# Zero fills by DMA, a wider yield rule for GpSimd, weights in small pieces, and other seeds in a planned attention kernel

## The chip, the cores and the metric

The kernel runs on one core of a Trainium2 chip. A core has five engines that run their own instruction streams and meet only at semaphores: TensorE (PE, matrix products), VectorE (DVE), ScalarE (ACT), GpSimd (POOL) and SyncE (SP, which here only issues DMAs). TensorE writes its results to PSUM, which has eight banks of 128 partitions by 512 floats. The metric is the device time of one launch in microseconds, taken as the median of several runs. A shorter time is better.

## The reference, cut to what matters

One sequence of S = 2048 rows of width D = 512 is normalised, goes through an attention with 32 query heads of width 16 over one shared key and value head, and through a two-layer network with F = 1792; the two results are multiplied and added to the input:

```python
xn = _layernorm(x)                                   # x = A_x, 2048 x 512
q, k, v = xn @ wq, xn @ wk, xn @ wv                  # 32 heads of 16; one k and one v head
p = softmax(einsum("bhqd,bkd->bhqk", q, k) * 16 ** -0.5)
s = einsum("bhqk,bkd->bhqd", p, v) @ wo
g = silu(silu(xn @ w1) @ w2)
out = x + s * g
```

The scores are 32 x 2048 x 2048 numbers. Each needs an exponential, and neither scores nor probabilities ever leave the chip's local memories.

## The kernel before, in words

**Units of work.** Queries are cut into four chunks of 512 columns, and keys into 32 blocks of 64. A *unit* is the score tile of one key block against one chunk of queries for four heads, 128 partitions by 512 columns, in one PSUM bank. There are 32 groups of 64 units, 2048 units in all. The matrix products run on quarters of the array: four matmuls of 64 x 32 weights run side by side and fill half of the array, so the planner speaks of two *lanes*. One such foursome is called a *half* here. Scores (L966, and L960 where the loaded weights are used again) go to lane 1. The products of probabilities with values (L1302), called PV here, take lane 0. Those of the network, of the queries and of the output (L704) use halves of both lanes.

**Two ways to take an exponential.** A unit goes one of two ways. In the *A way*, ScalarE computes exp straight out of PSUM, one unit or two neighbouring banks at a time (L1666), and the unit needs one PV entry. In the *D way*, VectorE turns the score into the bits of an approximate exponential in bf16 with one multiply and add (L1041), eight units make a batch, and three shifted copies of the batch are made with an integer addition on GpSimd (L1224) or, where allowed, on VectorE (L1220). The four versions are averaged by the weights in the values, so such a unit needs four PV entries. Two entries of the two column halves share one half-slot of lane 0.

**Prologue.** x arrives in four parts of four row tiles. VectorE computes the statistics (L538, L542), an inverse square root by a few small operations (L555 to L564) and the normalised tile xn (L567). TensorE transposes it (L606), ScalarE or VectorE copies it out (L616, L617), and keys (L632, evacuated at L650) and values (L669, evacuated at L678) follow for each part. Scores can only use keys that have been evacuated, and D units start only when all keys are there. The keys exist a second time, shifted by 16 rows (`kt_sb[:, 1]`), for the odd groups, and the queries a second time, shifted by 32 rows (`qt_sb[:, r, 1]`). The shifts are DMAs within local memory (L1348 on GpSimd's queue, L714 on SP's), and what they leave uncovered must be zero. The zeros come from GpSimd: four memsets of 128 x 512 (L500) and one of 16 x 2048 (L496). GpSimd also writes the constant columns of the values (L494). A tile of zeros for warming up TensorE is made by VectorE (L477) in the fourth output buffer.

**The order of the work** comes from a planner that runs when the kernel is built. Every operation is a task with an engine, an assumed duration, keys that it reads and writes, a priority and sometimes a gate. The planner keeps a clock for each engine, always advances the engine that is furthest behind, and lets it take the best task that is ready. What it places is fixed in that order in the engine's instruction stream, and waits are added for each dependency. TensorE has its own rule (`pe_step`), which weighs the backlog of ScalarE against that of VectorE to decide whether the next unit goes the A way or the D way. Its parameters are drawn anew for every 6 us of planned time from a list of seeds (`SEEDS`, `Mix.draw`); seed 0 means no deviation. A different list gives a different order everywhere.

**The shared port.** VectorE and GpSimd operations that are marked `ports=2` are never planned at the same time: the planner makes each wait for the last one of the other engine (`last2`, `locked`). In `avail`, GpSimd's two-port tasks also step back when a two-port VectorE task is about to be ready, but only if that task has no gate (`d.gate is None`):

```python
                if d.ports == 2 and d.gate is None and all(p.op is not None for p in d.preds) and (
                        self.ready(DV, d.reads, d.writes) <= self.clk[PO] + HOLD_PO):
                    return None
```

The xn operations (L567) have a gate: a tile may be overwritten only when the tile four before it has been transposed. The shifted copies on VectorE (L1220) have one too.

**Weights.** `w1` comes in one DMA after the sixth xn tile, `w2` in four DMAs and `wo` in one, each after a certain product of the network has been planned (`later`, `hidden`). All go through SP's queue.

Of the kernel before, what the change touches and what calls it, by code (L numbers as in the profile page):

```python
# [15 lines left out]
P = 128  # L16
# [3 lines left out]
W1_AT, SKIP = 5, 1877.999  # L20
T_ISSUE, T_SWDGE = 450.0, 1000.0
J_BASE, J_END, MIXJ = 0.114, 1.312, 2
SEEDS, STRETCH = [0, 0, 882634, 0, 348373, 328499, 78780, 554384, 89101, 903077, 320169, 0, 878569, 280070, 102111, 381856, 427096, 265022, 0, 740569, 0, 0, 0, 191854, 393933, 374197, 266972, 0, 665170, 0, 882882, 218695, 9227, 955074, 159633, 731624, 518155, 138034, 620799, 357599, 376984, 365473, 457970, 796664, 668429, 641664, 991272, 0, 0, 23990, 593814, 88565, 504692, 394759, 276845, 267858, 882770, 104810, 721623, 135503, 603776, 0, 337714, 100793, 638616, 0, 419715, 752789, 751312, 664693, 308960, 0, 762547, 276261, 218757, 897693, 0, 624478, 290921, 0, 713781, 335568, 417921, 100939, 814701, 0, 180062, 99721, 614963, 258262, 411291, 131548, 802432, 314922, 883804, 569039, 54637, 401726, 110613, 0, 983842, 914345, 0, 0, 0, 0, 0, 0, 0, 0], 6000.0
# [5 lines left out]
HOLD_PO = 394.351  # L29
# [3 lines left out]
Q_URG = 0.404  # L33
J_SLIP = 1.014
NEXT_OB, OB_SLACK = 8, 67.243
# [22 lines left out]
WIDE, PAIR_WAIT, GRP_WAIT = 2, 17.474, 124.091  # L58
Q_LEAD = 3.566
A_HIGH, D_HIGH, SLACK = 1856.266, 2005.987, 50.146  # L60
LEAD, CROWD, FRAG, DB_LOW = 296.727, 0.54, 0.993, 1
RUN, HOLD, PRESS = 6, 411.985, 18
ROOM = 1
START_Z, START_H, AHEAD, NEAR = 10, 14, 0.206, 11
CLOSING, URGENT, END_DV = 0, 4.336, 58
STARVED = 543.663
JLATE, JEVAC = 1.132, 1
MATE = 176.663
# [7 lines left out]
class Task:  # L76
    __slots__ = ("eng", "dur", "emit", "reads", "writes", "prio", "preds", "op", "on_place", "dma", "gate", "ports", "after", "ring", "first")

    def __init__(self, eng, dur, emit, reads=(), writes=(), prio=5, preds=(), on_place=None, dma=0, gate=None, ports=1):
        self.ports, self.after, self.ring = ports, None, None  # L80
        self.eng, self.dur, self.emit = eng, dur, emit
        self.reads, self.writes, self.prio = tuple(reads), tuple(writes), prio
        self.preds, self.on_place, self.dma, self.gate = [p for p in preds if p is not None], on_place, dma, gate
        self.op = None
# [11 lines left out]
class Planner:  # L96
# [122 lines left out]
    def avail(self, task):  # L219
# [5 lines left out]
        if task.eng == PO and task.ports == 2:  # L225
            for d in self.tasks[DV]:
                if d.ports == 2 and d.gate is None and all(p.op is not None for p in d.preds) and (
# [124 lines left out]
def bass_recurrent_scan__grouped_kv_mqa__dense_activation_silu__prompt_kernel(  # L352
# [29 lines left out]
    with ExitStack() as es:  # L382
# [75 lines left out]
        dma(SP, "wq", wq_sb[:], A_wq.rearrange("(dc p) n -> p dc n", p=P), 512, ["wq"], prio=0)  # L458
        for j in range(1, 4):
            dma(SP, "x", ds_sb[:, XB + 4 * j // BS, 4 * j % BS * NQ:(4 * j % BS + 4) * NQ].bitcast(BF16).rearrange("p (t d) -> p t d", d=D),  # L460
                xv[:, 4 * j:4 * j + 4, :], 512, [xkey(4 * j + h) for h in range(4)], prio=1)
        def later(task, which):
# [8 lines left out]
        for k, (f0, f1) in enumerate(((0, 4), (4, 8), (8, 11), (11, 14))):  # L471
            later(dma(SP, "w2", w2_sb[:, f0:f1, :], w2v[:, f0:f1, :], 128 * (f1 - f0), [("w2", k)], prio=3), hidden(0, k))
        wov = A_wo.rearrange("(o p) n -> p o n", p=P)
        later(dma(SP, "wo", wo_sb[:], wov, 512, ["wo"], prio=4), hidden(0, 4))

        pl.add(Task(DV, 60.0, lambda v: v.memset(scr_sb[:], 0.0), (), ["scr"], -1))
        pl.add(Task(DV, 550.0, lambda v: v.memset(zer_sb, 0.0), (), [("ob", 3)], 0))  # L477
# [15 lines left out]
        for j in range(K + 1):  # L493
            pl.add(Task(PO, T_MS, lambda g, j=j: g.memset(v_sb[:, j, :, DH:], 1.0 if j == 0 else SHIFT_W[j - 1]),  # L494
                        (), [("Vw", j)], 2, ports=2, gate=lambda: ("st", 0) in pl.lastw and ("st", 3) not in pl.lastw or xn_task[3].op is not None))
        pl.add(Task(PO, 1800.0, lambda g: g.memset(kt_sb[0:DH, 1, :], 0.0), [("xn", 3)], [("kt1", c) for c in range(NC)], 3,  # L496
                    gate=lambda: all(xn_task[t].op is not None for t in range(4)), ports=2))
        q1_fill = {}
        for r in range(NQR):
# [1275 lines left out]
```

## Time and profile before

| what | us |
|---|---|
| median of three runs (659.71 to 660.05) | 659.73 |
| the profiled execution | 660.8 |
| its span, first to last instruction | 658.8 |
| busy: TensorE, ScalarE, VectorE, GpSimd | 649.1, 641.5, 640.4, 571.2 |
| first exponential of the A way starts | 11.48 |
| first D evacuation on VectorE starts | 39.12 |
| last exponential ends | 649.1 |
| last output DMA is issued | 655.2 |

Three engines are busy for 97% of the span or more, so a share of busy time tells little. What counts is in which stretch each of them sits idle, and who it waits for then. The profile's matmul ends are modelled, so TensorE's busy time includes time in which only one of its lanes works. In the listings, the number in square brackets is the idle time of the engine ahead of the row, with what ended it. TensorE's clock was granted in full throughout.

### The profile page before, as it was taken

Reading aid. Unit: us, or ns where it says so; the run is one execution under the profiler, and the core shown is the slowest. Engines: PE = TensorE matmul, PEld = TensorE weight load, DVE = VectorE, ACT = ScalarE, POOL = GpSimd, SP = SyncE. Lnnn points to the kernel's source line nnn. Section 1 sums busy time; section 2 is a strip of 40 time slices with the busy share of each in tenths; the row PEclk is TensorE's granted clock in tenths of the full one; section 3 lists DMA queues with packets and bytes.
Section 4 is the critical chain, followed back from the end, with each engine's and each line's share of the span. In section 5 each row is a group of like instructions: output and inputs, shape, how many; then the busy total and the mean of one; then the engine's idle time right before and its main releaser. Section 6 shows DMA issues by size and latency. Waiting matters only on the chain.

```text
span 658.8 us, 44466 instructions
## 1 busy us (share of the span) xinstructions
PE 649.1 (99%) x22182; PEld 332.3 (50%) x19438; DVE 640.4 (97%) x1169; ACT 641.5 (97%) x1128; POOL 571.2 (87%) x320
## 2 busy tenths in 40 slices
PE   8999999999999999999999999999999999999997
PEld 3445555544555554544555554454445555554543
DVE  8999999999999999999999999999999999999976
ACT  6989999999999999999999999999999999999995
POOL 4038799999998978999999878999999998889891
PEclk9999999999999999999999999999999999999999
DMA  5314100000000010000000010000000000100001
GB/s 177 129 48 121 42 4 4 10 5 10 5 10 20 28 34 5 10 4 5 10 4 11 21 36 26 4 5 10 4 10 4 10 21 20 34 13 5 4 4 34
DMA packets 13432, 15.91 MB, mean 24 GB/s; under 512 B 2112, under 2 KB 12608, under 8 KB 13248
## 3 DMA queue, kind: packets, MB, share of 16 engines
q1 hardware_dynamic: 12768, 12.36, 6.2%
q8 instruction: 162, 2.65, 1.7%
q0 software_dynamic: 192, 0.46, 0.2%
q10 hardware_dynamic: 288, 0.26, 0.1%
q14 instruction: 22, 0.18, 0.1%
HBM read 8.95 MB, written 2.10 MB: 17 GB/s over the span
## 4 chain that ended last, share of the span: by engine, by line
PE 89%; ACT 5%; DVE 3%; POOL 1%; DMA 0%; issue 0%
PE ps L966 29%; PE ps L1302 24%; PE ps L704 21%; PE ps L960 14%; ACT pa_sb L1666 4%; DVE stats_sb L538 1%; DVE xn_sb L567 1%; PE ps L1510 0%; ACT t_sb L760 0%; DVE xnT_sb L617 0%; DMA kt_sb<-kt_sb 0%; POOL qt_sb L500 0%; POOL kt_sb L496 0%; DVE v_sb L678 0%; DVE kt_sb L650 0%
## 5 line engine op out<-in xcount | busy, mean ns | idle before, releaser
L1666 ACT ACTIVATE pa_sb<-ps 128x512 bf16<-128x512 f32 (+1 forms) x1038 | 610.6, 762 | 5.4 <-PE ps L966 4.4
L1224 POOL INT64_ADD ds_sb<-db_sb x300 | 562.2, 1897 | 43.7 <-DVE db_sb L1041 33.7
L1041 DVE TENSOR_SCALAR db_sb<-ps 128x512 uint16<-128x512 f32 x808 | 500.6, 679 | 5.5 <-PE ps L960 2.0
L966 PE MATMUL ps<-qt_sb,kt_sb 64*32 64x512 bf16 x5448 | 473.7, 378 | 1.9 <-DVE v_sb L678 0.8
L1302 PE MATMUL ps<-ds_sb,v_sb 64*32 64x512 bf16 x4848 | 352.1, 377 | 0.1
L1302 PE MATMUL ps<-pa_sb,v_sb 64*32 64x512 bf16 x2480 | 271.3, 377 | 0.7 <-DVE v_sb L678 0.5
L960 PE MATMUL ps<-qt_sb,kt_sb 64*32 64x512 bf16 x2744 | 265.7, 375 | 0.0
L966 PEld LDWEIGHTS ps<-qt_sb,kt_sb 64*32 64x32 bf16 x5448 | 132.3, 89 | 161.4 <-ACT pa_sb L1666 68.8
L1302 PE MATMUL ps<-db_sb,v_sb 64*32 64x512 bf16 x1616 | 211.8, 377 | 0.0
L1302 PEld LDWEIGHTS ps<-ds_sb,v_sb 64*32 64x32 bf16 x4848 | 134.1, 91 | 44.4 <-issue 15.8
L704 PE MATMUL ps<-xnT_sb,w_sb 64*32 64x512 bf16 x1792 | 135.4, 377 | 0.0
L704 PE MATMUL ps<-w_sb,u_sb 64*32 64x512 bf16 x1792 | 133.7, 376 | 0.0
L1302 PEld LDWEIGHTS ps<-pa_sb,v_sb 64*32 64x32 bf16 x2480 | 92.0, 91 | 28.2 <-issue 8.4
L1302 PEld LDWEIGHTS ps<-db_sb,v_sb 64*32 64x32 bf16 x1616 | 66.8, 91 | 16.5 <-issue 5.9
L704 PEld LDWEIGHTS ps<-xnT_sb,w_sb 64*32 64x32 bf16 x1792 | 43.8, 91 | 24.0 <-issue 6.5
L704 PEld LDWEIGHTS ps<-w_sb,u_sb 64*32 64x32 bf16 x1792 | 44.8, 91 | 20.3 <-issue 6.1
L760 ACT ACTIVATE t_sb<-ps 128x512 bf16<-128x512 f32 x72 | 47.8, 664 | 0.0
L761 DVE SCALAR_TENSOR_TENSOR u_sb<-t_sb,ps 128x512 bf16<-128x512 bf16 x56 | 37.9, 677 | 1.0 <-ACT t_sb L760 1.0
L704 PE MATMUL ps<-xnT_sb,wq_sb 64*32 64x512 bf16 x480 | 37.6, 378 | 0.0
L704 PE MATMUL ps<-wo_sb,on_sb 64*32 64x512 bf16 x384 | 30.8, 377 | 0.0
L1319 DVE STREAM_TRANSPOSE ps<-ps 128x512 f32<-128x512 f32 (+1 forms) x33 | 23.2, 705 | 3.3 <-PE ps L1302 3.3
L1348 POOL DMA_DIRECT2D kt_sb<-kt_sb x4 | 2.3, 566 | 21.2 <-DVE rstd_sb L558 7.8
(75 smaller groups left out, 193.4 us busy)
## 6 DMA issues: line engine op xcount, KB each, us to landing
xr_sb<-in_A_x_dram SPq DMA_DIRECT2D x16, 128.0 KB, 2.3
out_dram<-ob_sb SPq DMA_DIRECT2D x16, 128.0 KB, 1.7
w_sb<-in_B_w_dram SPq DMA_DIRECT2D x1, 1792.0 KB, 7.2
ds_sb<-in_A_x_dram SPq DMA_DIRECT2D x3, 512.0 KB, 6.6
qt_sb<-qt_sb SPq DMA_DIRECT2D x16, 96.0 KB, 2.5
w_sb<-in_B_w_dram SPq DMA_DIRECT2D x2, 512.0 KB, 4.7
w_sb<-in_B_w_dram SPq DMA_DIRECT2D x2, 384.0 KB, 3.3
wq_sb<-in_A_wq_dram SPq DMA_DIRECT2D x1, 512.0 KB, 4.8
```

What stands on the lines that cost most here:

```text
L538: ts_ = pl.add(Task(DV, 593.0, lambda v, t=t: v.bn_stats(stats_sb[:, t, :], x_tile(t)), [xkey(t)], [("st", t)], 1 + j, gate=(lambda j=j: S ...
L567: xn_task[i] = pl.add(Task(DV, 323.0, lambda v, i=i: v.tensor_scalar(xn_sb[:, i % 4, :], x_tile(i), mv_sb[:, i, 0:1], rstd_sb[:, i:i + 1], ...
L704: h = pe.matmul(bank(b)[32 * j:32 * (j + 1), :], lhsT=lhs(k, rows, 32 * j, 32), rhs=rhs(k, rows), start=first, stop=last, tile_position=(r ...
L760: t1 = Task(AC, T_AF + 0.8333 * NQ, lambda a: a.activation(t_sb[:, k, :], bank(b), ACT.Tanh, scale=scale), [("ps", b)], [("t", k)], 0)
L761: t2 = Task(DV, T_P, lambda v: v.scalar_tensor_tensor(out=dst, in0=t_sb[:, k, :], scalar=1.0, in1=bank(b), op0=ALU.add, op1=ALU.mult), [(" ...
L960: h = pe.add_instruction(mybir.InstMatmult(name=pe.bass.get_next_instruction_name(), engine=mybir.EngineType.PE, ins=[pe.lower_ap(q), pe.l ...
L966: h = pe.matmul(to, lhsT=keys, rhs=q, start=True, stop=True, tile_position=(r0, 32 * j), skip_group_check=True)
L1041: bt.P[k] = pl.add(Task(DV, T_P, lambda v: v.tensor_scalar(db_sb[:, bt.b, k * NQ:(k + 1) * NQ], bank(b), 128.0 * LOG2E, 128.0 * (SHIFT_BET ...
L1224: whole["po"].append(pl.add(Task(PO, T_P64, lambda g: g.int64_add(ds_sb[:, s, :].bitcast(U64), db_sb[:, bt.b, :].bitcast(U64), words), rea ...
L1302: h = pe.matmul(bank(OB)[q:q + 32, :], lhsT=lhs[rows], rhs=rhs[rows], start=s0, stop=s1, tile_position=(64 * l, q), skip_group_check=True)
L1319: t1 = pl.add(Task(DV, (T_TR - 60.0) / parts + 60.0, lambda v, cols=cols: v.transpose(bank(OB)[:, cols], bank(OB)[:, cols]), [("ps", OB)], ...
L1666: op = pl.place(AC, 0.8333 * NQ * n + T_AF, lambda a: a.activation(pa3[:, k0:k1 + 1:max(1, k1 - k0), :], ps3[:, b0:b1 + 1:step, :], ACT.Ex ...
```

## The change

Five things change.

1. The zeros for the second copies of queries and keys come from two DMAs on GpSimd's queue, which read VectorE's zero tile (`zeros`): 32 rows by 4 x 512 for the queries, and 16 rows by 4 x 512 for the keys. The five memsets at L500 and L496 go.
2. In `avail`, GpSimd steps back also for a two-port VectorE task with a gate, if the gate is open and the task isn't a shifted copy (`HOLD_G`, `shift`).
3. `w2` is loaded in 14 DMAs and `wo` in four, each behind a certain product; the loads of x for the output wait for other products.
4. The parameters of the planner are given with all their digits instead of three decimals.
5. The list of seeds is another one.

```diff
-W1_AT, SKIP = 5, 1877.999
+W1_AT, SKIP = 5, 1877.9992141310836
+HOLD_G = 1
...
-SEEDS, STRETCH = [0, 0, 882634, 0, 348373, ...], 6000.0
+SEEDS, STRETCH = [0, 281271, 540428, 919283, 237625, ...], 6000.0
...
         if task.eng == PO and task.ports == 2:
             for d in self.tasks[DV]:
-                if d.ports == 2 and d.gate is None and all(p.op is not None for p in d.preds) and (
+                if d.ports == 2 and all(p.op is not None for p in d.preds) and (d.gate is None or HOLD_G and not d.shift and d.gate()) and (
                         self.ready(DV, d.reads, d.writes) <= self.clk[PO] + HOLD_PO):
                     return None
...
+        def zeros(name, to, n, writes):
+            def emit(e):
+                return e.dma_start(to, zer_sb[to_rows, :].unsqueeze(1).to_broadcast([to_rows.stop - to_rows.start, n, NQ]))
+            to_rows = {"k": slice(0, DH), "q": slice(96, P)}[name]
+            return pl.add(Task(PO, T_SWDGE, emit, [("ob", 3)], writes, 0, [zero], dma=64 * 1024))
+
+        zero = pl.add(Task(DV, 550.0, lambda v: v.memset(zer_sb, 0.0), (), [("ob", 3)], 0))
...
+        q1_zero = zeros("q", qt_sb[96:P, :, 1, :], NQR, [("q1", r) for r in range(NQR)])
+        zeros("k", kt_sb[0:DH, 1, :].rearrange("p (c n) -> p c n", n=NQ), NC, [("kt1", c) for c in range(NC)])
...
-        for k, (f0, f1) in enumerate(((0, 4), (4, 8), (8, 11), (11, 14))):
-            later(dma(SP, "w2", w2_sb[:, f0:f1, :], w2v[:, f0:f1, :], 128 * (f1 - f0), [("w2", k)], prio=3), hidden(0, k))
+        for k in range(NFT):
+            later(dma(SP, "w2", w2_sb[:, k, :], w2v[:, k, :], 128, [("w2", k)], prio=3), hidden(0, max(0, k - 3)))
...
-        later(dma(SP, "wo", wo_sb[:], wov, 512, ["wo"], prio=4), hidden(0, 4))
+        for o in range(NOC):
+            later(dma(SP, "wo", wo_sb[:, o, :], wov[:, o, :], 128, [("wo", o)], prio=4), hidden(0, min(NFT - 1, 11 + o)))
...
-        pl.add(Task(DV, 550.0, lambda v: v.memset(zer_sb, 0.0), (), [("ob", 3)], 0))
...
-        pl.add(Task(PO, 1800.0, lambda g: g.memset(kt_sb[0:DH, 1, :], 0.0), [("xn", 3)], [("kt1", c) for c in range(NC)], 3,
-                    gate=lambda: all(xn_task[t].op is not None for t in range(4)), ports=2))
-        q1_fill = {}
-        for r in range(NQR):
-            q1_fill[r] = pl.add(Task(PO, T_MS, lambda g, r=r: g.memset(qt_sb[:, r, 1, :], 0.0), (), [("q1", r), ("qT", r, 1)], 2, ports=2,
-                        gate=lambda: ("st", 0) in pl.lastw and ("st", 3) not in pl.lastw or xn_task[3].op is not None))
+        q1_fill = {r: q1_zero for r in range(NQR)}
...
-                later(xr_task[tt], hidden(0, 5))
+                later(xr_task[tt], hidden(1, tt))
...
+            whole[DV].shift = True
```

## The prediction

> **What bounds the kernel now.** I read the page's busy times first, then the windows by stage, then ScalarE's rows at the start, then VectorE's and GpSimd's there. The page and the windows (time, then busy time and count of PE, PEld, DVE, ACT, POOL):
>
> ```profile
> PE 649.1 (99%) x22182; PEld 332.3 (50%) x19438; DVE 640.4 (97%) x1169; ACT 641.5 (97%) x1128; POOL 571.2 (87%) x320
> ...
> 11.48:38.75 27.27, 25.00 (x660) 12.32 (x604) 23.76 (x71) 23.77 (x39) 4.40 (x7) 1.00 0.26 87
> 38.75:73.00 34.25, 33.57 (x1117) 17.45 (x977) 33.01 (x56) 33.06 (x61) 25.02 (x15) 1.00 0.33 97
> 73.00:649.20 576.20, 575.95 (x20195) 295.44 (x17631) 568.98 (x975) 575.89 (x1011) 537.46 (x287) 1.00 0.04 12
> 649.20:658.80 9.60, 5.89 (x118) 2.82 (x102) 4.70 (x13) 2.77 (x5) 0.00 (x0) 1.00 0.17 56
> ```
>
> From 73.00 to 649.20 ScalarE is idle for 0.31 us of 576.20, while VectorE is idle for 7.2 us. So from 73 us on the time is ScalarE's work, plus 9.6 us of closing work behind its last exponential. ScalarE loses time only before 73 us, and its own rows say where:
>
> ```profile
> 11.48 14.20 ACT L1666 ACTIVATE pa_sb<-ps 128x512 bf16<-128x512 f32 x24 [0.50 <-PE ps L966]
> 26.37 4.14 ACT L1666 ACTIVATE pa_sb<-ps 128x1024 bf16<-128x1024 f32 x7 [0.69 <-PE ps L966]
> 31.37 1.57 ACT L1666 ACTIVATE pa_sb<-ps 128x512 bf16<-128x512 f32 x3 [0.85 <-PE ps L966]
> 33.65 2.64 ACT L1666 ACTIVATE pa_sb<-ps 128x1024 bf16<-128x1024 f32 x3 [0.71 <-PE ps L966]
> 36.18 0.60 ACT L760 ACTIVATE t_sb<-ps 128x512 bf16<-128x512 f32 x1
> 36.66 1.04 ACT L1666 ACTIVATE pa_sb<-ps 128x1024 bf16<-128x1024 f32 x1
> ```
>
> It runs without a break for 14.20 us and then waits for scores, because TensorE, which works in order, stands at transposes and keys that come from VectorE. At 38.75 the keys are complete and it starts again after 1.05 us. VectorE and GpSimd in that stretch:
>
> ```profile
> 14.88 0.83 DVE L678 TENSOR_TENSOR v_sb<-ps,wj_sb 128x640 bf16<-128x640 f32 x1 [0.37 <-PE ps L669]
> 16.44 1.38 DVE L567 TENSOR_SCALAR xn_sb<-ds_sb,mv_sb,rstd_sb 128x512 bf16<-128x512 bf16 x4 [0.74 <-POOL kt_sb L496]
> ...
> 14.61 1.79 POOL L496 MEMSET kt_sb<- 16x2048 bf16 x1 [1.66 <-DMA kt_sb<-kt_sb]
> ```
>
> VectorE carries the prologue (23.76 busy of 27.27), and 0.74 us of its idle time is the wait for GpSimd's memset.
>
> **The change, part by part.** I counted both kernels' instructions in the order in which they are issued. Unchanged: 1240 A units, 808 D evacuations, 21,696 matmuls of 32 x 512, 72 tanh. Total work hardly moves, so the question is when ScalarE gets it.
>
> *Memsets and yield.* The five memsets (1.93 + 1.79 us) leave GpSimd. VectorE now makes xn of tiles 4 to 7 directly behind the root: the last root operation starts at 14.34, the next follows 0.20 later, so xn starts at 14.54 instead of 16.44. Then it does two statistics (0.585 each) and the values (0.74) ahead of the two transposed copies (0.595 each), which end at 14.54 + 1.31 + 1.17 + 0.74 + 1.19 = 18.95 instead of 19.54. Two statistics, the keys, the root and the values later, xn of tiles 8 to 11 ends near 24.84 instead of 25.86. After that the order is the old one, and the shift of about 1.05 us lasts to the complete keys: 37.70 instead of 38.75. It can't be more than 3.5 us, VectorE's whole idle time in the stretch, and can be a loss of 0.5 if the fills delay x (below). I take 1.05, which adds up the rows of this very chain.
>
> *What TensorE issues meanwhile.* Before the transposes of tiles 4 to 7 stood 16 scores; now there are 9. TensorE waits for xn behind the ninth, until the last transposes end at about 16.8. ScalarE has done nine units by 15.9 and gets the tenth at about 17.3, so the unbroken run of 14.20 us gets a hole of 1.4 us. By the first tanh, ahead of the last keys, 45 units were done; now it is 38. By the last keys (L632, fourth part) TensorE has issued 47 scores; now it is 40. A unit costs ScalarE 0.482 us: busy 33.06 + 575.89 from 38.75 to 649.20, less 71 tanh at 0.48 (36.18 to 36.66), over the 1193 units left. So 7 x 0.482 = 3.37 us of work more stands behind the complete keys.
>
> *Order by the other seeds.* 195 pairs instead of 202 and 850 single exponentials instead of 836. A pair takes 212.2 / 202 = 1.05 us, two singles 2 x 444.6 / 836 = 1.064, so 0.1 more. Between first and ninth tanh ScalarE has 65 units in both kernels and lane 0 has 143 halves before, 141 after; I expect the 1.19 us of idle time there to stay. It could vanish (-1.2) or double (+1.2).
>
> *Shifted copies.* VectorE's three (1.22 us each) at the end go to GpSimd, 303 instead of 300 at 1.90. VectorE is idle for 6.2 us between 620 and 650 already, so its relief is worth nothing. GpSimd's 5.7 us lie beside lane 0: the last D score is issued 45 PV slots ahead of the end instead of 28, and 45 x 0.215 = 9.7 us covers three copies (5.7) and their use. If the cover were gone, the last copy would cost up to 1.9. From below, the closing work could shrink by the 0.8 us between last exponential and last PV (649.12 to 649.95). I take 0.
>
> *Fills and loads.* Two DMAs of 128 and 64 KB at 340 to 390 GB/s, which the DMA strip shows between 2 and 11 us, are 0.5 us of transfer among the loads of x. The first group of four tiles lands at 3.23 + 5.7 = 8.9 and is needed at 9.51, so 0.5 just fits; without that cover it costs 0.5. The query copy (L714) that waits for a fill goes out at 11.01, long after. On GpSimd the fills stand ahead of two value memsets, which ran from 3.30 to 4.29 and which VectorE's first two-port operation at 5.62 waits for; two issues at 0.57 from 1.6 on end by 2.8. Thirteen more weight loads at about 0.5 us each are on SP's queue. The second query copy (L714, issued at 43.42) stands behind three of them more and goes out 1.5 us later. It is first read by the 122nd score, at about 37.7 + 82 x 0.305 = 62.7 (0.305 us a score, 610.45 us over 2001 scores), so some 15 us cover it. None of these loads is on the path.
>
> Sum: -1.05 + 3.37 + 0.1 = +2.4 us. The profiled execution took 660.8 (span 658.8 and 2.0 around it), which becomes 663.2. It stands 1.07 above the median of 659.73, so the median becomes **662.1**.
>
> **A rule against the row.** TensorE's 99% comes with 50% of weight loads. Of lane 0, 2814 halves (2816 after) at 0.215 are 605 of the 634 us from the first PV at 15.98 to the last at 649.95, so by that count it is full to 95%. The Trainium skill (Perfetto Trace Analysis, Identifying the Most-Contended Engine) calls matmul busy time a poor measure and goes by the weight loads' share. By that rule TensorE has half its time free, the third rival has no chance, and the time is 662.1. By the lanes it has 5%, so I keep the rival.
>
> **The rivals.**
> 1. *The prologue closes up.* VectorE's 3.5 us of idle time all go, the complete keys come at 35.25, and the missing work is made good: -3.5 + 3.5 = 0, 659.7. If the later 1.19 and 0.31 go too, 658.2. For it: each gap in VectorE's rows follows TensorE, which now has fewer scores in the way. Against it: the root's eight steps stay 0.20 apart, and the tanh wait (0.82) isn't touched.
> 2. *VectorE is the bound (faster).* It is above 98% busy from 73 us on. It begins D work 1.05 earlier and has three copies of 1.22 less, 3.7 in all: 659.7 - 4.7 = 655.0. It decides if VectorE has no spare time in the end; against it stands its 6.2 us of idle time from 620 to 650.
> 3. *Lane 0 falls behind in the new order.* ScalarE then idles as between 38.75 and 73 (1.19 in 34.25, 3.5%) for another 100 us: +3.5, 665.6. For it: the lane is full to 95%. Against it: each stage's PV count after is within 3% of ScalarE's time, as before.
> 4. *The fills hold up GpSimd's queue.* If each kept GpSimd until it lands (2.9 us, as the key copy takes), the value memsets would end at 1.6 + 5.8 + 0.99 = 8.4 instead of 4.29, VectorE would stand 2.8 us at 5.62, and everything with it: 664.9. The rows speak against it: the key copy's own issue holds GpSimd for 0.57 only, and VectorE's operations from 1.5 to 3.3 us last 0.34 at most. The Trainium skill (SBUF — State Buffer, SBUF: two separate sides) has a rule for such a hold-up: a DMA from GpSimd's queue can't get its descriptors written while VectorE runs a two-port operation, and took 3.1 us instead of 0.62. By that figure the memsets end at 8.8, and the time is an estimated 665.3.
>
> **How the numbers follow.** Forecast 0.55 (660.6 to 663.6 by the shift of the keys and the idle time at 38.75 to 73), rival 1 0.20, rival 2 0.06, rival 3 0.14, rival 4 0.05. A measurement tells 0.2%, 1.3 us, from no change, so faster means below 658.4 and slower above 661.05. Faster: rival 2 and a fifth of rival 1, 0.10. Same: the rest of rival 1 and 0.08 of the forecast, 0.24. Slower: 0.66. The range 659.2 to 665.0 leaves out rival 2 and the outer parts of rivals 1 and 3.
>
> **What would show it.** Right: ScalarE's first unbroken run breaks at about 15.9 for 1 us or more; xn starts at 14.5 with no wait for GpSimd; 38 units by the first tanh, which starts near 35.1; from 73 us on ScalarE is idle for under 1 us; 9.6 us behind its last exponential. Wrong: a first tanh before 33, or an idle ScalarE in the middle.

## The result and the profile after

The changed kernel takes 660.90 us (median of 20 runs, 660.53 to 662.02), the kernel before 660.05 in the same runs (659.48 to 660.85). The ratio is 1.0012, with a 95% interval of 1.0007 to 1.0018: 0.85 us slower, a difference that the interval tells from zero but that is below the 0.2% of the prediction's classes. The forecast was 2.4 us slower, and its range of 659.2 to 665.0 holds the time. By the prediction's own classes this is no change, which it had given 0.24, against 0.66 for slower.

The page's busy times and the windows by stage of the profiled execution (660.56 us, span 658.7), with the columns of the windows shown before:

```profile
PE 649.5 (99%) x22181; PEld 342.4 (52%) x19502; DVE 636.4 (97%) x1166; ACT 641.4 (97%) x1135; POOL 574.4 (87%) x320
...
11.48:38.75 27.27, 24.07 (x668) 12.56 (x620) 25.02 (x73) 22.05 (x37) 2.15 (x4) 1.00 0.30 97
38.75:73.00 34.25, 34.25 (x1158) 17.66 (x1032) 34.19 (x60) 34.24 (x62) 27.01 (x15) 1.00 0.17 48
73.00:649.20 576.20, 575.83 (x20144) 305.32 (x17620) 562.72 (x967) 576.20 (x1021) 540.95 (x289) 1.00 0.05 15
649.20:658.80 9.60, 5.53 (x117) 2.27 (x106) 4.71 (x13) 2.84 (x6) 0.00 (x0) 1.00 0.17 57
```

ScalarE (fourth pair after the sum) does 22.05 us of work in the prologue where it did 23.77. In the next stretch it is busy for 34.24 of 34.25 us, where it was for 33.06, and from 73 us on for all of 576.20. The DMA share between 38.75 and 73 us (the number behind the clock) fell from 0.33 to 0.17. ScalarE's own rows at the start:

```profile
11.74 3.14 ACT L1674 ACTIVATE pa_sb<-ps 128x512 bf16<-128x512 f32 x4 [0.50 <-PE ps L973]
15.23 1.51 ACT L1674 ACTIVATE pa_sb<-ps 128x1024 bf16<-128x1024 f32 x2 [0.35 <-PE ps L973]
17.67 2.98 ACT L1674 ACTIVATE pa_sb<-ps 128x512 bf16<-128x512 f32 x5 [0.93 <-PE ps L973]
...
35.34 0.60 ACT L767 ACTIVATE t_sb<-ps 128x512 bf16<-128x512 f32 x1
35.83 1.08 ACT L1674 ACTIVATE pa_sb<-ps 128x512 bf16<-128x512 f32 x2
37.78 2.56 ACT L1674 ACTIVATE pa_sb<-ps 128x512 bf16<-128x512 f32 x5 [0.87 <-PE ps L973]
...
636.01 13.25 ACT L1674 ACTIVATE pa_sb<-ps 128x1024 bf16<-128x1024 f32 x17
```

A row joins neighbours of one line and names the shape of the first, so the count behind x is of operations, not of units. The run of 14.20 us without a break is gone: nine units with a short wait of 0.35 us among them, then 0.93 us of waiting. The first tanh starts at 35.34 instead of 36.18, and the exponentials behind the complete keys at 37.78 instead of 38.75. From there to the end of the last exponential (636.01 + 13.25 = 649.26) ScalarE's listing has no gap at all; before, it had several between 55 and 73 us:

```profile
56.11 0.60 ACT L1666 ACTIVATE pa_sb<-ps 128x512 bf16<-128x512 f32 x1 [0.35 <-PE ps L966]
...
69.23 1.74 ACT L1666 ACTIVATE pa_sb<-ps 128x512 bf16<-128x512 f32 x2 [0.19 <-PE ps L966]
...
72.44 1.94 ACT L1666 ACTIVATE pa_sb<-ps 128x1024 bf16<-128x1024 f32 x2 [0.49 <-PE ps L960]
```

VectorE's rows show why the keys come earlier:

```profile
14.60 0.16 DVE L571 SCALAR_TENSOR_TENSOR rstd_sb<-var_sb,rstd_sb 128x4 f32<-128x4 f32 x1
14.79 1.39 DVE L574 TENSOR_SCALAR xn_sb<-ds_sb,mv_sb,rstd_sb 128x512 bf16<-128x512 bf16 x4
```

The xn operation follows the root at once; before, it came at 16.44, behind the evacuation of the values, and had waited for GpSimd's memset. On GpSimd the two fills are issued in 0.72 and 0.53 us, and the value memsets behind them run when they ran before (3.29 instead of 3.30):

```profile
1.78 0.72 POOL L463 DMA_DIRECT2D qt_sb<-ob_sb  x1 [0.57 <-DVE row_sb L493]
2.50 0.53 POOL L463 DMA_DIRECT2D kt_sb<-ob_sb  x1
3.29 0.99 POOL L506 MEMSET v_sb<- 128x512 bf16 x2 [0.26 <-DVE part_sb L520]
```

### The profile page after: what moved, and what is told of

Read it like the earlier page. It is cut to its first block, busy times and chain, and to the rows that moved or that the text cites. A ratio compares the mean times of both kernels' runs of the same rounds, so it can differ in the third digit from the quotient of the medians.

```text
span 658.7 us, 44545 instructions
## 1 busy us (share of the span) xinstructions
PE 649.5 (99%) x22181; PEld 342.4 (52%) x19502; DVE 636.4 (97%) x1166; ACT 641.4 (97%) x1135; POOL 574.4 (87%) x320
## 3 DMA queue, kind: packets, MB, share of 16 engines
q8 instruction: 163, 2.67, 1.8%
## 4 chain that ended last, share of the span: by engine, by line
PE 84%; ACT 10%; DVE 4%; issue 0%
PE ps L1310 28%; PE ps L973 25%; PE ps L711 18%; PE ps L967 13%; ACT pa_sb L1674 9%; DVE stats_sb L545 1%; ACT t_sb L767 1%; DVE xn_sb L574 1%; DVE xnT_sb L624 0%; PE ps L1518 0%; PE ps L613 0%; DVE v_sb L685 0%; DVE kt_sb L657 0%; DVE var_sb L570 0%; DVE var_sb L568 0%; DVE mv_sb L549 0%
## 5 line engine op out<-in xcount | busy, mean ns | idle before, releaser
L1232 POOL INT64_ADD ds_sb<-db_sb x303 | 568.0, 1898 | 40.9 <-DVE db_sb L1048 24.6
L1310 PE MATMUL ps<-pa_sb,v_sb 64*32 64x512 bf16 x2480 | 267.0, 377 | 0.0
L1310 PE MATMUL ps<-db_sb,v_sb 64*32 64x512 bf16 x1616 | 208.4, 377 | 0.0
L711 PE MATMUL ps<-xnT_sb,w_sb 64*32 64x512 bf16 x1792 | 137.5, 377 | 0.2 <-DVE db_sb L1048 0.2
L711 PE MATMUL ps<-w_sb,u_sb 64*32 64x512 bf16 x1792 | 135.1, 376 | 0.2 <-ACT pa_sb L1674 0.2
L711 PEld LDWEIGHTS ps<-w_sb,u_sb 64*32 64x32 bf16 x1792 | 43.2, 91 | 20.1 <-issue 7.4
L1356 POOL DMA_DIRECT2D kt_sb<-kt_sb x4 | 2.2, 538 | 25.5 <-DVE kt_sb L657 9.1
```

The source lines that it names most:

```text
L711: h = pe.matmul(bank(b)[32 * j:32 * (j + 1), :], lhsT=lhs(k, rows, 32 * j, 32), rhs=rhs(k, rows), start=first, stop=last, tile_position=(r ...
L1232: whole["po"].append(pl.add(Task(PO, T_P64, lambda g: g.int64_add(ds_sb[:, s, :].bitcast(U64), db_sb[:, bt.b, :].bitcast(U64), words), rea ...
L1310: h = pe.matmul(bank(OB)[q:q + 32, :], lhsT=lhs[rows], rhs=rhs[rows], start=s0, stop=s1, tile_position=(64 * l, q), skip_group_check=True)
```

## The experiments

Each kernel ran beside the kernel before on the same chip, and a ratio is that of the two. Where a held order is spoken of, the edit is made behind the planner, so every other instruction stays where it was; `put` sets one operation more at a place of an engine's order.

**Which of the five parts do anything to the order.** The planner gives the order of the changed kernel, instruction for instruction, also with `HOLD_G = 0`: once the memsets are gone, the wider yield rule finds nothing to yield. With the old weight loads it gives the same order on the four computing engines too. The digits of the parameters do count: with three decimals, as before, the planner gives the changed kernel another order, in which 162 pairs of units share an exponential where the changed kernel has 195. So the order differs from that of before by the memsets' leaving, by the digits and by the seeds, and no run here changes the digits alone.

### The weight loads

The first experiment takes the small pieces back, and the first loads of x for the output with them, which then go out earlier again:

```diff
-        for k in range(NFT):
-            later(dma(SP, "w2", w2_sb[:, k, :], w2v[:, k, :], 128, [("w2", k)], prio=3), hidden(0, max(0, k - 3)))
+        for k, (f0, f1) in enumerate(((0, 4), (4, 8), (8, 11), (11, 14))):
+            later(dma(SP, "w2", w2_sb[:, f0:f1, :], w2v[:, f0:f1, :], 128 * (f1 - f0), [("w2", k)], prio=3), hidden(0, k))
...
+        later(dma(SP, "wo", wo_sb[:], wov, 512, ["wo"], prio=4), hidden(0, 4))
...
-                later(xr_task[tt], hidden(1, tt))
+                later(xr_task[tt], hidden(0, 5))
```

> The changed kernel with w2 loaded in four DMAs, wo in one and the loads of x for the output where they were; its order on TensorE, ScalarE, VectorE and GpSimd is that of the changed kernel, instruction for instruction. Theory: the loads are covered, so 660.9 us, within 0.4, and the same start of the exponentials behind the keys (37.8). Rival (the small loads delay the second query copies or the first products on TensorE): a gap of ScalarE between 38 and 73 us appears or goes, 0.5 us or more.

Measured: 662.84 us, ratio 1.0050 (1.0038 to 1.0063), against 1.0012 with the pieces. The pieces and the later loads of x together are worth 0.38%, 2.5 us, in this order. The theory of covered loads falls. ScalarE's rows in its trace:

```profile
59.68 2.00 ACT L1673 ACTIVATE pa_sb<-ps 128x1024 bf16<-128x1024 f32 x3 [0.17 <-PE ps L966]
...
64.06 2.09 ACT L1673 ACTIVATE pa_sb<-ps 128x512 bf16<-128x512 f32 x3 [0.41 <-PE ps L972]
...
67.50 2.64 ACT L1673 ACTIVATE pa_sb<-ps 128x512 bf16<-128x512 f32 x4 [0.37 <-PE ps L972]
```

TensorE's own row ahead of the second of these gaps:

```profile
62.95 0.39 PE L1309 MATMUL ps<-db_sb,v_sb 64*32 64x512 bf16 x1 [0.51 <-issue]
```

Gaps like those of before are back, 0.95 us in all. TensorE itself stood idle ahead of 62.95 for 0.51 us and, by "issue", waited for nothing that the profile names: no data, no bank, no weight. The start times of the 72 tanh tell where the time is lost: up to 56.5 us they lie 0.1 earlier than in the changed kernel, at 65 us 0.97 later, at 82 us 1.46 later, and from there to the end the difference stays between 1.41 and 1.46. So all that this execution loses (it is the fastest of the five) arises while the weights and x are loaded, and nothing later makes it good. The four loads of x go out from 63.34 us on, behind TensorE's gap at 62.95, so about 1.1 of the 1.5 us come from a time in which only weights were on their way. The rest, the gap at 67.50, can't be told apart.

The opposite experiment gives the kernel before the small pieces and leaves the rest as it was (the same edit the other way round, and `later(xr_task[tt], hidden(1, tt))`).

> The kernel before with the weight loads in small pieces and the later loads of x, as in the changed kernel; its order on TensorE, ScalarE, VectorE and GpSimd is that of before, instruction for instruction. Theory (large weight transfers hold up TensorE, which then waits for nothing that the profile names): ScalarE's idle time between 38.75 and 82 us (1.5 us in the profiled execution of before, 0 in that with the fills) is 0, and the median falls by 0.5 to 1.0 us. Rival (that idle time comes from the order of the work): the idle time and the median stay. Second rival (the pieces matter only in the order of the changed kernel): median within 0.2 us of before.

Measured: 658.24 us (658.12 to 658.71) against 659.34 for before; ratio 0.9983 (0.9974 to 0.9992). It is faster than both kernels, by 1.1 us than before and by some 1.9 than the changed kernel (1.0012 / 0.9983 = 1.0029). Its window from 38.75 to 73 us, with the columns as before:

```profile
38.75:73.00 34.25, 34.25 (x1168) 17.36 (x1012) 34.10 (x59) 34.15 (x63) 26.32 (x15) 1.00 0.18 55
```

The only row of ScalarE between 37 and 82 us that has idle time ahead of it, and its last row of exponentials:

```profile
38.85 8.80 ACT L1667 ACTIVATE pa_sb<-ps 128x512 bf16<-128x512 f32 x16 [1.05 <-PE ps L967]
...
633.87 13.19 ACT L1667 ACTIVATE pa_sb<-ps 128x1024 bf16<-128x1024 f32 x17
```

ScalarE's idle time between 38.75 and 73 us falls from 1.19 to 0.10 us with the order held; behind 38.85 no gap of 0.15 us or more is left. The gain is a little above the 0.5 to 1.0 us of the theory, and both rivals fall. That the loads cost this time is shown; by what way they do is the next question.

Do such transfers hurt by their data being awaited, or by their mere traffic? The third experiment adds traffic that nobody waits for:

```diff
+        seen = [[o for o in pl.order[PE] if "mk_T" in o.emit.__qualname__][-1]]
+        for k in range(4):
+            seen = [put(SP, 31 + k, lambda e: e.dma_start(xn_sb[:], w2v[:, 0:4, :]), seen, 512 * 1024)]
+        pl.order[AC][600].deps += seen
```

The last line makes ScalarE's 600th operation wait for them, some 200 us after they have landed.

> The changed kernel with four transfers of 512 KB more, one behind the other, from about 106 us on, into a tile that nobody reads then; nothing on the way waits for them. Theory (large transfers hold up TensorE's stream): between 106 and 125 us TensorE has idle times of 0.2 us or more that end with no release, and the exponentials behind come 0.3 to 1.5 us later. Rival (such transfers cost nothing; in the loads' time somebody waits for the data): no such rows, and 660.9.

Measured: 662.24 us, ratio 1.0041 (1.0028 to 1.0055), 1.9 us more than the changed kernel. TensorE's rows there:

```profile
111.52 0.37 PE L1310 MATMUL ps<-pa_sb,v_sb 64*32 64x512 bf16 x1 [1.14 <-issue]
119.80 0.37 PE L1310 MATMUL ps<-pa_sb,v_sb 64*32 64x512 bf16 x1 [0.22 <-issue]
```

And ScalarE's:

```profile
111.99 8.32 ACT L1674 ACTIVATE pa_sb<-ps 128x512 bf16<-128x512 f32 x14 [0.90 <-PE ps L973]
120.67 1.57 ACT L1674 ACTIVATE pa_sb<-ps 128x512 bf16<-128x512 f32 x3 [0.36 <-PE ps L973]
```

TensorE stands for 1.14 and 0.22 us in the middle of these transfers, again with nothing that it waits for, and the tanh behind are 2.1 us later, more than the 0.3 to 1.5 us expected. So traffic can do it without anyone waiting for its data. This was the slowest of five executions (660.84 to 663.69 us), and the changed kernel would take 660.1 us beside these runs of before (1.0012 times 659.34), so the cost differs from 0.7 to 3.6 us from one execution to the next. What TensorE lacks then was not shown. The trace has a DMA queue of the kind "instruction" (5 packets and 0.08 MB in these 20 us), so its own instructions arriving late behind the transfers is a possible reason, but this is only argued, and one figure speaks against it: the packets' own transfer time is not longer (1.7% of the engines' time, 1.8% without the transfers).

In the other kernels, too, the effect is not the same in every execution. The kernel before shows 1.5 us of these gaps in the profiled execution of 660.8 us, and none behind the keys in the one with the two fills added (below, 659.04 us), though it loads the weights in the same large transfers. So the medians carry the argument here, more than the single profiles. The pieces don't exclude it either: one later profile of a variant with pieces (the halved D evacuations below) has gaps of 0.34 and 0.31 us at 66.9 and 71.3 us.

### The seeds

```diff
-SEEDS, STRETCH = [0, 281271, 540428, ...], 6000.0
+SEEDS, STRETCH = [0, 0, 882634, 0, 348373, ...], 6000.0
```

> The changed kernel with the list of seeds of before. Theory (ScalarE's work decides): its order has 1248 A units in 154 pairs and 940 single exponentials, against 1240 in 195 and 850. At 1.05 and 0.532 us that is 661.8 us of exponentials against 657.0, 4.8 more; and 38 units instead of 40 stand ahead of the last keys, 1.0 more behind them. So 660.9 + 5.8 = 666.7 us, with ScalarE idle for under 1 us from 73 us on. Rival (VectorE is the bound): it has 800 D evacuations instead of 808 and becomes faster by about 5 us, 656. Rival (the order does not matter): 660.9.

Measured: 670.13 us, ratio 1.0161 (1.0147 to 1.0175), 9.8 us more than the changed kernel; 5.8 had been expected. ScalarE idles for 0.24 of the 619.61 us from the keys to its last exponential, so that part of the theory holds:

```profile
38.46:658.07 619.61, 619.42 (x21250) 324.07 (x18474) 598.66 (x1022) 619.37 (x1132) 556.19 (x297) 1.00 0.06 16
```

The price of the exponentials was off. I had taken a pair at 1.05 us and two singles at 1.064, from the rows' total times divided by their number. But rows overlap, and the distance from one start to the next is what counts. From 35.34 to 35.83 above, a single operation takes 0.49. A pair takes 0.92, which rows of the experiment with sixteen halved exponentials (below) show:

```profile
46.98 1.02 ACT L1674 ACTIVATE pa_sb<-ps 128x1024 bf16<-128x1024 f32 x1
47.90 0.72 ACT L1731 ACTIVATE pa_sb<-ps 128x256 bf16<-128x256 f32 x2
```

So a pair saves 0.06 us against two singles. With these two distances, from the first exponential behind the keys to the end of the last:

| kernel | singles, pairs, tanh | 0.49, 0.92, 0.49 us each | measured |
|---|---|---|---|
| before, with pieces | 807, 193, 71 | 607.8 | 608.2 |
| changed | 822, 189, 71 | 611.4 | 611.5 |
| changed, old seeds | 914, 148, 71 | 618.8 | 619.6 |

The absolute match owes something to luck, since 0.005 us on a single is 4 us; the differences (3.7 and 7.4, measured 3.3 and 8.1) don't depend on it. Each of these three orders is as long as ScalarE's work in it. And a list of seeds that serves one kernel need not serve another: the changed kernel with the list that served the kernel before loses 9.8 us.

This run also shows how much of the earlier keys hangs on the seeds. The xn operation for tiles 4 to 7 starts as early as in the changed kernel (14.67 us), but the exponentials behind the keys start at 38.46, only 0.4 us earlier than in the kernel before with pieces, where the changed kernel gains 1.07.

### The fills

```diff
+        for rows, to, fills in ((slice(0, DH), kt_sb[0:DH, 1, :].rearrange("p (c n) -> p c n", n=NQ), k_fill), (slice(96, P), qt_sb[96:P, :, 1, :], q_fill)):
+            early = put(PO, 2, lambda e, rows=rows, to=to: e.dma_start(to, zer_sb[rows, :].unsqueeze(1).to_broadcast(
+                [rows.stop - rows.start, 4, NQ])), [pl.order[DV][4]], 64 * 1024)
+            for o in fills:
+                o.deps.append(early)
```

> The kernel before with the two fills as DMAs added at the place that they have in the changed kernel; the memsets stay, so the order is that of before. Theory (the fills' transfers delay the first loads): the first exponential at 11.7 us instead of 11.48, the last keys and the end later by the same 0.26: 660.3 us. Rival (the later start comes from something else): first exponential at 11.48 and 660.05 us. Rival 4 of the prediction (a fill holds GpSimd until it lands): value memsets end at about 8 us and the time rises by 3 us or more.

Measured: 659.42 us against 659.36, ratio 1.0003 (0.9994 to 1.0012). The value memsets run at 3.30, so rival 4 falls here too. The first exponential starts at 11.80, as the theory has it, but the restart behind the keys only at 38.91, 0.06 later than in the kernel with pieces and 0.16 later than in the profile of before. The first exponentials of the eleven profiles with early fills lie between 11.54 and 11.87, those of the two profiles without fills at 11.48 and 11.57. The fills cost the start some 0.2 us in the mean, though the two ranges overlap, and the end nothing that can be measured.

```diff
+        fills = pl.order[PO][2:4]
+        pl.order[PO][2:4] = []
+        pl.order[PO][4:4] = fills
...
+        fills[0].deps.append(pl.order[SP][6])
```

> The changed kernel with the two fills issued behind the first two value memsets, when the x tiles 8 to 11 have landed. Theory (the fills delay the first loads): first exponential at 11.48 instead of 11.74, exponentials behind the keys at 37.5 instead of 37.8, 660.6 us. Rival: no change, 11.74 and 660.9.

Measured: 663.13 us, ratio 1.0060 (1.0047 to 1.0072). The first exponential does come earlier (11.41), but both sides missed what follows. The wait that I added stands in GpSimd's queue, and the rest of that queue stands behind it:

```profile
10.79 0.72 POOL L463 DMA_DIRECT2D qt_sb<-ob_sb  x1 [6.51 <-DMA ds_sb<-in_A_x_dram]
11.51 0.53 POOL L463 DMA_DIRECT2D kt_sb<-ob_sb  x1
12.02 1.48 POOL L506 MEMSET v_sb<- 128x512 bf16 x3
14.53 0.55 POOL L1356 DMA_DIRECT2D kt_sb<-kt_sb  x1 [1.03 <-DVE var_sb L570]
```

The first key copy (L1356) goes out at 14.53, TensorE waits 3.37 us for it ahead of its ninth score, and the keys are complete 4.0 us later (exponentials from 41.78). About half of that is this wait, in place of one of 1.03 us; much of the rest is TensorE's clock (last section). In this profile all 72 tanh stay 4.0 us later to the end.

### Which engine sets the time behind the keys

The prediction priced each unit that is missing at the keys by ScalarE's time for it. The first test gives ScalarE that time back:

```diff
+            def activation(self, to, src, f):
+                return self.a.activation(to[:, :, :NQ // 2], src[:, :, :NQ // 2], f)
...
+        for o in single[:16]:
+            o.emit = lambda a, f=o.emit: f(Half(a))
```

> The changed kernel with 16 single exponentials behind the complete keys over 256 columns instead of 512 (the other half of their probabilities is stale): 16 x 256 columns are 3.4 us of ScalarE's work, that of the seven units that the new prologue does less. Theory (every unit that is missing at the keys costs its full time, since ScalarE alone bounds the rest): 3.4 us less, 657.5 us against 660.9 (ratio to before 0.996), no idle time of ScalarE behind the keys. Rival (TensorE's lane 0 is close behind): ScalarE idles again between 38 and 82 us and the gain is 2 us or less.

Measured: 660.51 us, ratio 1.0017 (1.0008 to 1.0026): nothing gained. The theory falls. What the rival foretold came, but the rows only say that scores came late, not that lane 0 was the reason. ScalarE's rows show it waiting for scores between the shortened exponentials, with six gaps of 0.16 to 0.26 us up to 48.9 us, three of them in these rows:

```profile
39.38 0.38 ACT L1731 ACTIVATE pa_sb<-ps 128x256 bf16<-128x256 f32 x1 [0.26 <-PE ps L973]
40.01 1.02 ACT L1674 ACTIVATE pa_sb<-ps 128x1024 bf16<-128x1024 f32 x1 [0.25 <-PE ps L967]
...
48.89 2.62 ACT L1674 ACTIVATE pa_sb<-ps 128x512 bf16<-128x512 f32 x4 [0.26 <-PE ps L973]
```

By 51.5 us it is back at its old times. One stretch might be special, so the next three take some 7 us from one engine each, spread over the run. They use one helper, which halves the columns of so many operations, picked at even distances between two places of an engine's order; each kernel has one of the three calls:

```diff
+        halve(AC, lambda o: "act_step" in o.emit.__qualname__ and cell(o, "b0") == cell(o, "b1"), 32, 120, 1080)
...
+        halve(PE, lambda o: "do_pv" in o.emit.__qualname__ and len(cell(o, "mm")) == 2, 64, 400, 5200)
...
+        halve(DV, lambda o: "db_sb" in o.emit.__code__.co_freevars and "tensor_scalar" in o.emit.__code__.co_names and "ds_sb" not in o.emit.__code__.co_freevars, 28, 300, 1090)
```

> The changed kernel with 32 single exponentials over 256 columns instead of 512, spread evenly from about 80 to 630 us (the other half of these probabilities is stale). A halved one saves 0.22 us by the rows of the sixteen (0.60 to 0.38), 7.0 in all. Theory A (ScalarE bounds the middle of the run; the sixteen brought nothing because TensorE paced that one stretch): 6 to 7 us less, 654. Theory B (the engines run in lock step by the fixed order, and none alone is the bound): less than half of it, 658 to 661. Theory C or D (lane 0 of TensorE, or VectorE, is the bound): nothing.

> The changed kernel with 64 PV half-slots of lane 0 over 256 columns instead of 512, spread evenly over the same time (these products are incomplete): 64 x 0.108 us, 6.9 us less work in lane 0. Theory C (lane 0 is the bound): 6 to 7 us less. Theory A (ScalarE) and D (VectorE): within 0.5 us of 660.9. Theory B (lock step): 0.5 to 3 us less.

> The changed kernel with 28 D evacuations over 256 columns instead of 512, spread evenly over the same time (the other half is stale): about 28 x 0.25 us, 7 us less work on VectorE. Theory D (VectorE is the bound, rival 2 of the prediction): 6 to 7 us less. Theory A and C: within 0.5 us of 660.9. Theory B (lock step): 0.5 to 3 us less.

Measured, as ratios to before, where the changed kernel has 1.0012:

| 7 us less on | median | ratio (95%) |
|---|---|---|
| ScalarE | 659.77 | 0.9997 (0.9987 to 1.0006) |
| TensorE, lane 0 | 661.09 | 1.0015 (1.0006 to 1.0025) |
| VectorE | 661.19 | 1.0020 (1.0010 to 1.0031) |

ScalarE's 7 us bring 1.0; the other two bring nothing. None of the three alone is the bound. That is theory B's claim, but its figure came out for ScalarE only: for the other two it had named 0.5 to 3 us. GpSimd, busy for 540.95 of 576.20 us, was not shortened in any run, and no run shortened all four engines at once. In the profile of the changed kernel the other engines wait for GpSimd for 2.3 us in all, so little speaks for it as the bound, but it is not ruled out.

Where the rest of ScalarE's 7 us went does not show as idle time: from 73 to 640 us ScalarE is busy for 565.26 us where the changed kernel has 567.00. Its groups by shape (columns: count, busy us, mean ns of one, idle time ahead), first in the changed kernel:

```profile
L1674 ACT ACTIVATE pa_sb<-ps 128x512 bf16<-128x512 f32 x850 | 452.4, 694 | 5.0 <-PE ps L973 4.9
```

The kernel with 32 halved exponentials:

```profile
L1674 ACT ACTIVATE pa_sb<-ps 128x512 bf16<-128x512 f32 x818 | 436.0, 656 | 5.6 <-PE ps L973 4.9 <-PE ps L1310 0.2 <-PE ps L967 0.2
...
L1730 ACT ACTIVATE pa_sb<-ps 128x256 bf16<-128x256 f32 x32 | 15.3, 478 | 0.0
```

An exponential that stands alone shows 0.60 us, and a halved one 0.38. In the mean they show 656 to 694 and 478 ns. So a row can be longer than its work, and ScalarE looks busy without a gap; whether the operation was held up or overlaps its neighbours, the rows don't say. The Trainium skill (Perfetto Trace Analysis, Identifying the Most-Contended Engine) calls the occupancy of ScalarE a fair measure of how close it is to its limit. Here it shows 576.20 of 576.20 us, and ScalarE lost 7 us of work for 1.0 us of time, so the measurement decides against it.

The last test of this kind shortens 32 whole A units: score, exponential and PV entry, each over 256 columns:

```diff
+            o.emit = lambda e, f=o.emit: f(Half(e))
+            s.emit = lambda e, f=s.emit: f(Half(e))
+            p.emit = lambda e, f=p.emit, j=j, n=len(cell(p, "mm")): f(Part(e, j, n))
```

Here `o`, `s` and `p` are a unit's exponential, its score and its PV half-slot; `Part` halves only this unit's entry.

> The changed kernel with 32 A units over 256 columns instead of 512, spread evenly from about 80 to 630 us, in all three of their operations: scores, exponential and PV entry (their results are incomplete). That is the work of 16 whole units, on TensorE and on ScalarE at once. The prediction's price (0.482 us for each unit that is left behind the keys): 7.7 us less, 653. Theory B (lock step by the fixed order; the exponentials alone brought 1 us of their 7, lane 0 alone nothing): more than the exponentials alone, but less than half of the price, 1 to 4 us. If it is 1 us or less, the price of a unit in a held order is near nothing, and the 3.3 us that the changed kernel takes longer behind the keys belong to the order as a whole, not to seven units' work.

Measured: 659.55 us (658.47 to 660.60), ratio 0.9996 (0.9986 to 1.0005), 1.1 us less than the changed kernel and no more than the exponentials alone had brought, which is at the edge between the two cases that the expectation told apart. In the profiled execution the tanh move from 0.22 us earlier at the start to 2.03 at 602 us, so 16 units' work is worth 1.8 us there, in one of the fastest of twelve executions: 0.11 us for a unit. The price of 0.482 is not what a unit costs in a held order.

One kernel adds work instead, ten operations on VectorE:

```diff
+            put(DV, at, lambda v: v.tensor_scalar(
+                wke_sb[:].rearrange("p k e -> p (k e)")[:, :480].rearrange("p (c n) -> p c n", n=16), rstd_sb[:].unsqueeze(1).to_broadcast([P, 30, 16]),
+                1.0, 1.0, op0=ALU.mult, op1=ALU.add), last)
```

> The changed kernel with ten operations more on VectorE, of 480 columns each, spread over the middle of the run (about 0.55 us each, 5.5 in all); their results aren't used. Theory (ScalarE is the bound, VectorE has 13 us of idle time from 73 us on): within 0.3 us of 660.9, and ScalarE's idle time from 73 us on stays under 0.5. Rival 2 of the prediction (VectorE is the bound): 5 us more, 666.

Measured: 669.41 us, ratio 1.0150 (1.0135 to 1.0166), 9.1 us more than the changed kernel. The ten operations took longer than I had meant, 0.47 to 2.97 us and 11.8 in all; at least the longest of them ran beside GpSimd's additions (last section). But of these 11.8 us, 9.1 reach the end, although VectorE has 13.5 us of idle time from 73 us on. Its idle time is no reserve: it lies at other places than the delay. VectorE being as critical as the others when it is late says nothing for rival 2, since work taken from it brought nothing.

## Why the prediction was right, and where it was wrong

Direction and range were right, and the size was off by 1.5 us: 2.37 forecast, 0.85 measured, little more than a third. The kernel before with pieces allows the steps to be read one by one, because neither it nor the changed kernel has gaps of ScalarE behind the keys in its profile. The first three rows are read from these two profiles, the last two from the medians; they add up to 0.8. The last two have intervals of some 0.6 us either way, so that the sum meets the measured 0.85 this closely is luck:

| step | forecast | measured |
|---|---|---|
| complete keys earlier | -1.05 | -1.07 (38.85 to 37.78) |
| longer from there to the last exponential | 3.37 + 0.1 | 3.27 (608.21 to 611.48) |
| behind the last exponential | 0 | -0.30 (9.74 to 9.44) |
| fills | 0 | 0.0 (ratio 1.0003) |
| small pieces of the weights, later loads of x | 0 | -1.1 (ratio 0.9983) |

- **What bounds the kernel.** Wrong as put. "From 73 us on the time is ScalarE's work" fits the length of each planned order within 0.8 us, but taking 7 us of that work away brought 1.0. ScalarE is busy for the largest share there, but taking work from it, from lane 0 or from VectorE alone moved the end by 1.0 us at most. That the planner has packed the engines too tightly for one of them to give way alone is the likely reason, not a shown one.
- **Memsets and yield.** Right, 1.07 for 1.05, with xn at 14.79 less some 0.25 for a start that was late in this execution. The earlier xn belongs to the memsets; the yield does nothing. That all of the shift lasts to the complete keys belongs to this list of seeds: with the old list only 0.4 us arrive there.
- **What TensorE issues.** The observations came nearly as told: the first tanh at 35.34 with 38 units done, and the break behind the ninth unit, though at 16.74 instead of 15.9 and for 0.93 us instead of 1.4, with a shorter wait of 0.35 us ahead of it. The size fits as well, but its reason does not hold, so the match may be luck. A unit cost 0.11 us in a held order, not 0.482, and TensorE was level again at 73 us: by the counts of the windows it issued 828 matmuls up to 40 us and 1120 from 40 to 73 us, in the changed kernel and in the kernel with pieces alike. Behind that it fell back, by 24 matmuls up to 150 us and by 56 up to 350. That the order was 3.3 us longer is measured; whether seven units at the start made it so, or the way this list of seeds went, stays open.
- **Order by the other seeds.** This step failed in one sentence: "I expect the 1.19 us of idle time there to stay." It went, and the pieces with the later loads of x took it.
- **Fills and loads.** The step that failed. "None of these loads is on the path" is true of their data, which nobody waited for. Their traffic was on the path: TensorE stood while they ran, and the change removes 1.1 us of that (2.5 in its own order). The profile of before had the sign in it, an idle time of TensorE that ends with "issue", among DMAs at a share of 0.33, and I read only ScalarE's rows there:

```profile
55.68 0.39 PE L966 MATMUL ps<-qt_sb,kt_sb 64*32 64x512 bf16 x2 [0.46 <-issue]
```

  A second sign was that the profiled execution stood 1.07 us above the median: it contained 1.5 us of gaps, which the execution with the fills, in the same order, does not have. I carried them into the forecast as a property of the order.
- **Shifted copies.** Right: 303 copies on GpSimd, none on VectorE, and the end is 0.3 us shorter, not longer.
- **The rivals.** The prologue did not close up (1): VectorE is still idle for 2.25 us in it. Work taken from VectorE brought nothing (2). Lane 0 fell nowhere behind ScalarE (3): ScalarE has no idle time from 37.78 us on. The fills did not hold GpSimd (4), and the Trainium skill's hold-up of a DMA's descriptors (SBUF — State Buffer, SBUF: two separate sides) doesn't show here: their issues took 0.72 and 0.53 us, beside VectorE operations of 0.33 us at most.

## What to carry to other kernels

When a transfer is large, ask not only who waits for its data but also what its traffic may hold up; an idle engine whose gap ends with no release is the place to look, and cutting the transfer into pieces, or moving it, is a cheap try. In a kernel that a planner has packed to the last us, an engine that is busy all the time is not therefore the one to relieve: shorten some of its operations and see whether the end moves, before pricing a change by its busy time. And when the profiled execution stands well above the median, find out which of its gaps are only its own.

## What the hardware showed besides

- **TensorE's clock after a pause.** In the kernel with the late fills TensorE stood idle for 3.37 us ahead of 16.79 us, and the granted clock (the number ahead of the last two) fell to half for about six microseconds:

```profile
15.00:17.00 2.00, 0.21 (x4) 0.14 (x4) 1.96 (x6) 0.00 (x0) 0.08 (x1) 0.87 0.31 95
17.00:19.00 2.00, 2.00 (x66) 1.67 (x64) 0.78 (x2) 1.51 (x2) 0.00 (x0) 0.50 0.90 240
19.00:21.00 2.00, 2.00 (x28) 1.78 (x30) 1.52 (x2) 0.00 (x0) 0.00 (x0) 0.50 1.04 426
21.00:23.00 2.00, 2.00 (x29) 0.80 (x34) 1.93 (x5) 1.18 (x3) 0.00 (x0) 0.50 0.65 257
23.00:27.00 4.00, 4.00 (x136) 2.01 (x122) 2.27 (x12) 3.36 (x6) 0.54 (x1) 0.96 0.07 20
```

  The values and transposes for the next tiles (L676, L613) then take 1.88 and 1.89 us, where they take 1.18 and 1.07 in the changed kernel, and ScalarE's next hole, ahead of 21.63, is 2.67 us long instead of 0.93. The Trainium skill (TensorE: Matmul & The Clock Gate, Part 1: The HAM clock gate) has half the clock after an idle window of about 3.4 us, and this trace agrees.
- **VectorE beside GpSimd.** One of the ten operations added on VectorE, 480 columns from memory to memory, shows 2.97 us where the shortest of them shows 0.47. GpSimd's integer additions, 1.9 us each, ran from 290.60 to 294.41:

```profile
291.71 2.97 DVE L1736 TENSOR_SCALAR wke_sb<-rstd_sb 128x480 bf16<-128x480 f32 x1
```

  That GpSimd held it up fits these times, which end 0.3 us apart, but no run takes GpSimd's additions away. The planner's own operations of this kind are kept apart by the `ports=2` rule, which the added ones went around.
